# Two groups per slot for q and PV in slots 8 to 27, and the second quad's output weights prepared later

## The chip, the cores and the metric

The kernel runs on one core of a Trainium2 chip. A core has a matrix engine (PE, whose weight loads are listed apart as PEld), a vector engine (DVE), a scalar engine (ACT), a general engine (POOL), and queues that start DMA transfers (SP issues nearly all of them here). Every engine takes its instructions strictly in the order in which they were written, and waits at the head of its list until what the next instruction needs is there. The metric is the time of one execution in microseconds (us).

## The reference

One transformer block with adaptive layer norm: an attention part, a gated feed-forward part, and a modulation vector from `c`.

```python
mod = (_silu(c) @ w_mod).reshape(c.shape[0], 6, 1, -1)
h = _layernorm(x) * (1 + ca) + sa              # x: 2048 rows of 512
q = (h @ wq)                                   # 32 heads of 128
scores = q @ k.T * (128 ** -0.5)               # 8 k/v heads, the last 512 keys
o = softmax(scores) @ v
x = x + ga * (o @ wo)                          # wo: 4096 x 512
h = _layernorm(x) * (1 + cb) + sb
x = x + gb * ((_gelu(h @ w_gate) * (h @ w_up)) @ w_down)
```

All inputs are float32. The kernel computes each float32 product as three float16 matmuls: both operands are split into a high and a low half, and high·high, high·low and low·high are added up in PSUM. One such triple is called a group below.

## The kernel before

**Slots and units.** The attention part is cut into 512 slots. Slot t computes one tile of scores, 128 queries by 512 keys, for one head; four slots are a unit (one head, 512 queries), four units a set (two heads, two query blocks), and eight sets of four units make one half of the rows. The loop over t at the end of the attention part writes one slot after the other, and each slot writes to all engines.

**What a slot writes.** `scores(t)` is one group on PE into a PSUM bank `ps`; there are two such banks, so the scores of slot t need the bank that the exponentials of slot t-2 have read. `peak(t)` is the row maximum on DVE (`nm`). `expo(t)` is the exponential on ACT (`ee`), with the row sums. In odd slots ACT scales the sums of two slots (`rr`), and DVE takes their reciprocal in the slot after. `high(t-2)` on ACT writes the high half of the normalised probabilities, `low(t-3)` on DVE the low half (both called `p`), and SP then starts the DMA that transposes them into `pt`.

**What fills PE.** After the scores, a slot takes groups off a queue called `work`: q projections (`pq`, four groups for a unit), the product of probabilities and values (PV, `po`, four groups for a unit, of the unit two before), and from slot 30 on output projections (`py`). How many it takes is `EARLY[t]` for the first slots and 3 after them. In slots 8 to 27 each unit puts eight groups in the queue, so before the change its four slots take 3, 3, 2 and 0. When a `pq` or a `po` is complete, ACT writes the high half of its float16 split (`qt` or `ot`, line 747) at the start of the next slot, ahead of that slot's exponential, and DVE the low half (line 748) behind that slot's maximum. The same pair of instructions splits `w` and `k` where they are needed early.

**Banks.** Eight PSUM banks: two for `ps`, one called `qa`, and five (`acc`) that are handed round among `pq`, `po`, `py`, small sums (`pst`) and, in slots that the table `PSE` names, the exponentials `ee`; in the other slots `ee` lies in SBUF. A new tile waits for the last reader of the one that had its bank.

**Output weights.** A quad is four heads, whose rows of `wo` get one scale. `wo_items` loads each tile, lets ACT take its sum of squares (`sumsq`, line 219), lets `o_spread` turn the four sums into a scale on POOL and DVE, loads the tile again, and lets POOL multiply it and split it into halves (lines 657, 159 and 160) and SP store it. The slots are those of `WOS` (sums of squares) and `WOP` (the multiplication), counted from the quad's first set; the second quad counts from slot 32. POOL prepares the `w` tiles of each set in the same way (`set_steps`, lines 163, 159, 160 and 806).

Of the kernel before, what the change touches and what calls it, by code (L numbers as in the profile page):

```python
# [52 lines left out]
NPT = 3  # L53
NE = 6
CB = (11, 27)
PSE = dict.fromkeys((5, 7, 8, 9, 14, 18, 19, 21, 22, 23, 25, 26, 27), "acc") | dict.fromkeys((11, 15, 20, 24, 28), "qa")
EARLY = (2, 2, 0, 0, 2, 2, 0, 0)
WOS = ((6, 7, 8, 9), (-9, -8, -6, -5), (-16, -15, -14, -13))
WOP = ((17, 19, 20, 22), (10, 12, 16, 17), (-6, -4, 10, 12), (-6, -4, -3, -2))
SETPOS = (20, 14, 13, 12, 10, 8)  # L60
SETPOS2 = (18, 12, 11, 10, 9, 7)
TAIL = 12
# [3 lines left out]
def block_kernel(ctx: ExitStack, tc: tile.TileContext, x, kT, v, wq, wo, wg, wu, wd, cT, wc, wm, out):  # L66
# [8 lines left out]
    def tmp(name):  # L75
        return pool.tile([P, 512], F32, tag="e", name=name, bufs=NE)
# [7 lines left out]
    def bank(tag, name, bufs):  # L84
        return psum.tile([P, 512], F32, tag=tag, name=name, bufs=bufs)
# [7 lines left out]
    acc, moved, bg = {}, [0], []  # L93
# [61 lines left out]
    def halves(dst, src, act=False):  # L155
        if act:
            nc.scalar.activation(dst[:, 0, :], src, AF.Copy)
        else:
            nc.gpsimd.tensor_scalar(dst[:, 0, :], src, 1.0, 1.0, op0=ALU.mult, op1=ALU.mult)
        nc.gpsimd.tensor_tensor(dst[:, 1, :], src, dst[:, 0, :], op=ALU.subtract)  # L160

    def times(t, by):
        nc.gpsimd.tensor_scalar(t, t, by, 1.0, op0=ALU.mult, op1=ALU.mult)
# [15 lines left out]
    def col(name, i=0):  # L179
        return ST[name][:, i:i + 1]  # L180
# [7 lines left out]
    def little(name, n=1, bufs=4, dtype=F32):  # L188
        return small.tile([P, n], dtype, tag=name, name=name, bufs=bufs)
# [27 lines left out]
    def sumsq(out, src):  # L217
        with nc.allow_low_precision(reason="only a scale follows from it, which the margin in norm2 covers"):
            nc.scalar.activation(junk, src, AF.Square, scale=PRE, accum_out=out)
# [6 lines left out]
    def norm2(out, m, n, by, ps=None):  # L226

        ps = ps or sums(m, n)
        if n == 1:
            ts(out, ps[:, 0:1], TINY, None, ALU.max)  # L230
        elif n == 2:
            ts(out, ps[:, 0:1], TINY, ps[:, 1:2], ALU.max, ALU.add)
        else:
            nc.vector.tensor_reduce(out, ps[:, 0:n], axis=AX.X, op=ALU.add)
            pool_ts(out, out, TINY, 1.0, ALU.max)
        nc.gpsimd.tensor_tensor(out, out, half_, op=ALU.pow)  # L236
        pool_ts(out, out, by * 1.005 / PRE)

    def pool_ts(out, src, a, b=1.0, op0=ALU.mult, op1=ALU.mult):
        nc.gpsimd.tensor_scalar(out, src, a, b, op0=op0, op1=op1)  # L240

    def then(fn, d=3):

        if now[0] < 0:
            fn()
        else:
            at(("d", now[0] + d), fn)
# [29 lines left out]
    def y_scale(qd):  # L277
        pool_ts(col("ysc", qd), col("ysc", qd), col("vmax", qd), 1.0 / TOP15)

    def o_spread(qd, m, more):  # L280
        w = col("ysc", qd)
        norm2(w, m, 4, 1.0)
        pool_ts(w, w, col("gam", 0), 1.0 / TOP14)
        pool_ts(w, w, 1e-30, 1.0, ALU.max)

        def second():
            nc.vector.reciprocal(col("osc", qd), w)
            if qd == 0:
                y_scale(qd)
            more()  # L290

        then(second)
# [332 lines left out]
    def get_v():  # L625
        return pair("v16", "v16", 2)
# [7 lines left out]
    def reader(src):  # L634
        st = {}

        def load():
            st["r"] = raw("raw")
            dma(st["r"], src)

        return st, load

    def wo_items(qd, ts_, tp):
        m = {}
        for k in range(4):
            h = 4 * qd + k
            src = wo[h * P:(h + 1) * P, :]
            st, load = reader(src)
            sp, load_again = reader(src)

            def stat(st=st, k=k):
                if not m:
                    m["m"] = little("lm", 4, dtype=BF16)
                sumsq(m["m"][:, k:k + 1], st["r"])

            def parts(sp=sp, h=h):
                nc.gpsimd.tensor_tensor(sp["r"], sp["r"], m["g"], op=ALU.mult)
                WO[0, h] = get_wo()
                halves(WO[0, h], sp["r"])

            if qd == 0:
                def load_kept(st=st, sp=sp, src=src):
                    st["r"] = sp["r"] = pool.tile([P, D], F32, tag="wo", name="wor", bufs=8)
                    dma(st["r"], src)

                at(3 + k, load_kept)
                at(("w", ts_[k]), stat)
                at(("w", tp[k]), parts)
            else:
                sched(ts_[k], (load, [stat]))  # L670
                sched(tp[k], (load_again, [parts]))
            at(tp[k] + 5, lambda h=h: store(("wo", h), WO[0, h]))

        def more():
            m["g"] = pool.tile([P, D], F32, tag="gs", name="gs", bufs=1)
            pool_ts(m["g"], rows[2], col("osc", qd))

        def spread():
            o_spread(qd, m["m"], more)

        at(("w", ts_[3] + (4 if 1 < qd < 7 else 3)), spread)
# [25 lines left out]
    def v_items(g):  # L707
        st, load = reader(v[g])
        m = {}

        def stat():
            m["m"] = little("lm", 4, dtype=BF16)
            sumsq(m["m"][:, 0:1], st["r"])

        def spread():
            w = little("lw", 1, 2)
            norm2(col("vmax", g), m["m"], 1, 1.0)
            pool_ts(w, col("vmax", g), 1.0 / TOP14)
            if g:
                y_scale(g)  # L720
            then(lambda: nc.vector.reciprocal(col("vsc", g), w), 3 if g > 1 else 2)

        def parts():
            KV[0, g, 1] = get_v()
            times(st["r"], col("vsc", g))
            halves(KV[0, g, 1], st["r"])

        return load, stat, spread, parts
# [13 lines left out]
    def run(key):  # L742
        for fn in later.pop(key, []):
            fn()
# [248 lines left out]
    def expo(t):  # L993
        e = bank(PSE[t], "ee", NACC if PSE[t] == "acc" else 1) if t in PSE else tmp("ee")
        if t % 2 == 0:
            sm = small.tile([P, 2], F32, name="sm", bufs=4)
        else:
            sm = E[t - 1]["sm"]
        nc.scalar.activation(e, E[t]["ps"], AF.Exp, bias=E[t]["nm"], scale=1.0, accum_out=sm[:, t % 2:t % 2 + 1])  # L999
        E[t].update(e=e, sm=sm)  # L1000
# [217 lines left out]
    for g in range(NG):  # L1218
        half, pr = divmod(g, NPR)
        t0 = 16 * g  # L1220
        qd = pr // 2
# [21 lines left out]
        else:  # L1243
# [12 lines left out]
            if pr % 2 == 0:  # L1256
                wo_items(qd, [t0 + o + (qd == 7) for o in WOS[min(qd, 2)]], [t0 + o for o in WOP[min(qd, 2) + qd // 6]])

# [302 lines left out]
    with tc.manual_schedule():  # L1561
        begin()
        nexty, invs = [], {}
        for t in range(T + TAIL):
# [27 lines left out]
            run(("x", t))  # L1592
            for _ in range(4 if t >= T else EARLY[t] if t < len(EARLY) else 3):
                if t in (4, 5):
# [245 lines left out]
```

## Time and profile before

| | us |
|---|---|
| median of 3 runs | 1733.63 (1732.84 to 1733.82) |
| the profiled execution, and its span | 1734.19, and 1732.4 |
| PE busy in the span | 1711.2 (99%) |
| DVE, ACT, POOL busy | 1425.8 (82%), 1254.3 (72%), 1093.3 (63%) |
| scores of slot 8, of slot 28 and of slot 30 start at | 45.18, 92.28 and 98.35 |

The 1.8 us between the profiled execution and its span lie outside the recorded instructions. In a list of instructions in order of time, the first number of a row is its start from the span's start, the second its duration; a bracket at the end gives the idle time of that engine just before, and what ended it. Three matmuls of a group are listed as x3 and overlap, so that six of them, listed as 1.46 us, take 1.29 us from start to start.

### The profile page before, as it was taken

Reading aid. Unit: us, or ns where it says so; the run is one execution under the profiler, and the core shown is the slowest. Engines: PE = TensorE matmul, PEld = TensorE weight load, DVE = VectorE, ACT = ScalarE, POOL = GpSimd, SP = SyncE. Lnnn points to the kernel's source line nnn. Section 1 sums busy time; section 2 is a strip of 40 time slices with the busy share of each in tenths; the row PEclk is TensorE's granted clock in tenths of the full one; section 3 lists DMA queues with packets and bytes.
Section 4 is the critical chain, followed back from the end, with each engine's and each line's share of the span. In section 5 each row is a group of like instructions: output and inputs, shape, how many; then the busy total and the mean of one; then the engine's idle time right before and its main releaser. Section 6 shows DMA issues by size and latency. Waiting matters only on the chain.

```text
span 1732.4 us, 26343 instructions
## 1 busy us (share of the span) xinstructions
PE 1711.2 (99%) x8012; PEld 787.1 (45%) x8012; DVE 1425.8 (82%) x2476; ACT 1254.3 (72%) x2819; POOL 1093.3 (63%) x1328
## 2 busy tenths in 40 slices
PE   7999999999999999999999999999999999999998
PEld 5444444444444444444444444444444444444444
DVE  7888898988888899888888888888896788676666
ACT  6988788888888777897787777787785354455442
POOL 4879778777788884655665755747760345735424
PEclk9999999999999999999999999999999999999999
DMA  7999999999999998999999999999997556355353
GB/s 234 218 208 210 214 214 205 225 205 220 211 229 222 206 210 181 219 207 224 198 232 219 206 231 208 203 218 221 229 227 164 163 145 196 118 164 174 96 157 104
DMA packets 693454, 343.51 MB, mean 198 GB/s; under 512 B 579136, under 2 KB 602688, under 8 KB 693312
## 3 DMA queue, kind: packets, MB, share of 16 engines
q1 hardware_dynamic: 693024, 341.30, 85.4%
q8 instruction: 63, 1.03, 0.3%
q14 instruction: 79, 0.65, 0.1%
q10 hardware_dynamic: 288, 0.52, 0.1%
HBM read 137.50 MB, written 63.70 MB: 116 GB/s over the span
## 4 chain that ended last, share of the span: by engine, by line
PE 86%; DVE 5%; ACT 4%; POOL 2%; DMA 2%; issue 1%; SPq 0%; POOLq 0%; DVEq 0%; ACTq 0%
PE py L91 18%; PE po L91 17%; PE ps L91 16%; PE fa L91 8%; PE qa L91 8%; PE fc L91 4%; PE qc L91 4%; PE ya L91 3%; PE fb L91 2%; PE qb L91 2%; PE yc L91 2%; ACT ee L999 1%; DVE p L1016 1%; DVE nm L990 1%; ACT p L1011 1%
## 5 line engine op out<-in xcount | busy, mean ns | idle before, releaser
L999 ACT ACTIVATE ee<-ps,nm 128x512 f32<-128x512 f32 x512 | 349.6, 683 | 184.2 <-DVE nm L990 181.0
L1016 DVE SCALAR_TENSOR_TENSOR p<-ee,rr,p 128x512 f16<-128x512 f32 x512 | 454.1, 887 | 8.1 <-ACT p L1011 7.5
L990 DVE TENSOR_REDUCE nm<-ps 128x1 f32<-128x512 f32 x512 | 350.3, 684 | 105.7 <-PE ps L91 102.9
L91 PE MATMUL ps<-k,qt 128*128 128x512 f16 x1536 | 414.9, 379 | 3.8 <-ACT ee L999 2.5
L1011 ACT ACTIVATE p<-ee,rr 128x512 f16<-128x512 f32 x512 | 363.9, 711 | 21.9 <-DMA pt<-p 11.6
L91 PE MATMUL po<-pt,v 128*128 128x512 f16 x1536 | 372.9, 379 | 2.8 <-DVE kmax L184 1.0
L91 PE MATMUL py<-wo,ot 128*128 128x512 f16 x1536 | 371.3, 379 | 0.0
L91 PEld LDWEIGHTS <-w 128*128 128x128 f16 x2184 | 214.0, 98 | 259.7 <-issue 2.7
L91 PEld LDWEIGHTS <-v 128*128 128x128 f16 x1536 | 149.9, 98 | 185.1 <-issue 5.1
L91 PEld LDWEIGHTS <-ot 128*128 128x128 f16 x1536 | 150.3, 98 | 181.2
L91 PEld LDWEIGHTS <-qt 128*128 128x128 f16 x1536 | 145.8, 98 | 174.8 <-issue 3.3
L1320 POOL TENSOR_TENSOR fg<-fg 128x512 f32<-128x512 f32 x48 | 63.0, 1312 | 147.0 <-DVE fg L1294 144.2
L748 DVE SCALAR_TENSOR_TENSOR ot<-po,ot 128x512 f16<-128x512 f32 x128 | 87.8, 686 | 37.7 <-ACT ot L747 37.3
L1304 ACT ACTIVATE at<-fg 128x512 f16<-128x512 f32 x92 | 56.3, 626 | 80.1 <-DVE fg L1294 61.7
L999 ACT ACTIVATION_READ_ACCUMULATOR ee<-ps,nm 128x1 f32 x512 | 100.1, 195 | 0.0
L960 DVE SCALAR_TENSOR_TENSOR acc<-py,ysc,acc 128x512 f32<-128x512 f32 x128 | 94.7, 740 | 5.3 <-PE py L91 5.3
L91 PE MATMUL qa<-t,w 128*128 128x512 f16 x348 | 84.9, 379 | 0.0
L236 POOL TENSOR_TENSOR lw<-lw,half__86 128x1 f32<-128x1 f32 x39 | 25.0, 641 | 91.0 <-DVE lw L186 91.0
L91 PE MATMUL fa<-t,w 128*128 128x512 f16 x336 | 81.7, 379 | 0.1
L747 ACT ACTIVATE ot<-po 128x512 f16<-128x512 f32 x128 | 73.9, 577 | 5.0 <-PE po L91 5.0
L403 POOL TENSOR_TENSOR rs<-rs,nhalf 128x1 f32<-128x1 f32 x32 | 18.7, 586 | 92.9 <-DVE rs L397 90.0
L91 PEld LDWEIGHTS <-wo 128*128 128x128 f16 x504 | 49.3, 98 | 60.6 <-issue 1.3
(243 smaller groups left out, 2821.9 us busy)
## 6 DMA issues: line engine op xcount, KB each, us to landing
w<-kept SPq DMA_DIRECT2D x123, 256.0 KB, 3.3
wo<-kept SPq DMA_DIRECT2D x72, 256.0 KB, 3.3
kept<-stage SPq DMA_DIRECT2D x67, 256.0 KB, 3.2
raw<-in_wo SPq DMA_DIRECT2D x56, 256.0 KB, 3.2
kept<-w SPq DMA_DIRECT2D x39, 256.0 KB, 3.3
rw<-in_wq SPq DMA_DIRECT2D x38, 256.0 KB, 3.1
hs<-hf SPq DMA_DIRECT2D x32, 256.0 KB, 2.8
pt<-p SPq DMA_TRANSPOSE x512, 3.5
```

The costliest lines, as they stand in the source:

```text
L91: nc.tensor.matmul(ps, a, b, start=first and n == 0, stop=last and n == 2, skip_group_check=chain)
L236: nc.gpsimd.tensor_tensor(out, out, half_, op=ALU.pow)
L403: nc.gpsimd.tensor_tensor(st["rs"], st["rs"], nhalf, op=ALU.pow)
L747: nc.scalar.activation(t[:, 0, :], src, AF.Copy, scale=scale)
L748: return lambda: nc.vector.scalar_tensor_tensor(t[:, 1, :], src, scale, t[:, 0, :], op0=ALU.mult, op1=ALU.subtract)
L960: nc.vector.scalar_tensor_tensor(acc[ti], st["p"], by, acc[ti], op0=ALU.mult, op1=ALU.add)
L990: nc.vector.tensor_reduce(nm, E[t]["ps"], axis=AX.X, op=ALU.max, negate=True)
L999: nc.scalar.activation(e, E[t]["ps"], AF.Exp, bias=E[t]["nm"], scale=1.0, accum_out=sm[:, t % 2:t % 2 + 1])
L1011: nc.scalar.activation(p16[:, 0, :], E[t]["e"], AF.Copy, scale=E[t]["r"])
L1016: nc.vector.scalar_tensor_tensor(p16[:, 1, :], E[t]["e"], E[t]["r"], p16[:, 0, :], op0=ALU.mult, op1=ALU.subtract)
L1304: nc.scalar.activation(t[:, 0, :], g, AF.Copy)
L1320: nc.gpsimd.tensor_tensor(g[o], g[a], g[b], op=ALU.subtract)
```

## The change

`EARLY` is continued with twenty 2s: slots 8 to 27 take two groups each. `WOS` and `WOP` get other slots for the second quad: its sums of squares move from slots 23, 24, 26 and 27 to 35, 36, 38 and 39, its multiplications from 42, 44, 48 and 49 to 47, 49, 52 and 53. The second quad's `ysc` is then multiplied by `vmax` where the first's is, in `o_spread`. `PSE` names other slots; among others 6, 12, 13, 16 and 17 now have their `ee` in PSUM, and 8, 11, 14 and 15 in SBUF.

```diff
-EARLY = (2, 2, 0, 0, 2, 2, 0, 0)
+EARLY = (2, 2, 0, 0, 2, 2, 0, 0) + (2,) * 20
-PSE = dict.fromkeys((5, 7, 8, 9, 14, 18, 19, ...), "acc") | dict.fromkeys((11, 15, 20, 24, 28), "qa")
+PSE = dict.fromkeys((5, 6, 7, 9, 13, 17, 18, 19, ...), "acc") | dict.fromkeys((12, 16, 20, 24, 28), "qa")
-WOS = ((6, 7, 8, 9), (-9, -8, -6, -5), (-16, -15, -14, -13))
+WOS = ((6, 7, 8, 9), (3, 4, 6, 7), (-16, -15, -14, -13))
-WOP = ((17, 19, 20, 22), (10, 12, 16, 17), (-6, -4, 10, 12), (-6, -4, -3, -2))
+WOP = ((17, 19, 20, 22), (15, 17, 20, 21), (-6, -4, 10, 12), (-6, -4, -3, -2))
@@ o_spread, second()
             nc.vector.reciprocal(col("osc", qd), w)
-            if qd == 0:
+            if qd < 2:
                 y_scale(qd)
@@ v_items, spread()
-            if g:
+            if g > 1:
                 y_scale(g)
```

PE's order differs only up to slot 33; ACT's, DVE's, POOL's and SP's up to about slot 56. Three places show how.

ACT from the exponential of slot 22 to that of slot 25, before:

```order
L999 ACTIVATE ee,sm<-ps,nm 128x512
L1011 ACTIVATE p_1100<-ee,rr 128x512
L747 ACTIVATE ot<-po 128x512
L999 ACTIVATE ee,sm<-ps,nm 128x512
L1004 ACTIVATE rr<-sm 128x2
L1011 ACTIVATE p_1130<-ee,rr 128x512
L219 ACTIVATE junk,lm<-raw 128x512
L999 ACTIVATE ee,sm<-ps,nm 128x512
L1011 ACTIVATE p_1149<-ee,rr 128x512
L747 ACTIVATE k<-raw,ksc 128x512
L219 ACTIVATE junk,lm<-raw 128x512
L999 ACTIVATE ee,sm<-ps,nm 128x512
```

and the same stretch now:

```order
L999 ACTIVATE ee,sm<-ps,nm 128x512
L1011 ACTIVATE p_1089<-ee,rr 128x512
L999 ACTIVATE ee,sm<-ps,nm 128x512
L1004 ACTIVATE rr<-sm 128x2
L1011 ACTIVATE p_1117<-ee,rr 128x512
L747 ACTIVATE ot<-po 128x512
L999 ACTIVATE ee,sm<-ps,nm 128x512
L1011 ACTIVATE p_1143<-ee,rr 128x512
L747 ACTIVATE k<-raw,ksc 128x512
L999 ACTIVATE ee,sm<-ps,nm 128x512
```

The two sums of squares are gone, and the `ot` split stands ahead of the exponential of slot 24, no longer of slot 23.

DVE from the maximum of slot 23 to the `k` split of slot 25, before (`p_1149` is the low half of slot 22):

```order
L990 TENSOR_REDUCE nm<-ps 128x1
L748 SCALAR_TENSOR_TENSOR ot<-po,ot 128x512
L1016 SCALAR_TENSOR_TENSOR p_1100<-ee,rr,p_1100 128x512
L990 TENSOR_REDUCE nm<-ps 128x1
L1007 RECIPROCAL rr<-rr 128x2
L1016 SCALAR_TENSOR_TENSOR p_1130<-ee,rr,p_1130 128x512
L990 TENSOR_REDUCE nm<-ps 128x1
L1016 SCALAR_TENSOR_TENSOR p_1149<-ee,rr,p_1149 128x512
L748 SCALAR_TENSOR_TENSOR k<-raw,ksc,k 128x512
```

and now (`p_1143` is the low half of slot 22):

```order
L990 TENSOR_REDUCE nm<-ps 128x1
L1016 SCALAR_TENSOR_TENSOR p_1089<-ee,rr,p_1089 128x512
L990 TENSOR_REDUCE nm<-ps 128x1
L748 SCALAR_TENSOR_TENSOR ot<-po,ot 128x512
L1007 RECIPROCAL rr<-rr 128x2
L1016 SCALAR_TENSOR_TENSOR p_1117<-ee,rr,p_1117 128x512
L990 TENSOR_REDUCE nm<-ps 128x1
L1016 SCALAR_TENSOR_TENSOR p_1143<-ee,rr,p_1143 128x512
L748 SCALAR_TENSOR_TENSOR k<-raw,ksc,k 128x512
```

The `ot` split moved from an odd slot to an even one, where the reciprocal and a low half stand behind it. Slots 12, 16 and 20 show the same.

POOL around slots 48 to 54, where it makes the `w` tiles of the fifth set (`w_2145` before, `w_2143` now), before:

```order
L657 TENSOR_TENSOR raw<-raw,gs 128x512
L159 TENSOR_SCALAR wo<-raw 128x512
L160 TENSOR_TENSOR wo<-raw,wo 128x512
L240 TENSOR_SCALAR qsc<-lt 128x1
...
L806 TENSOR_TENSOR rw<-rw 128x256 x4
L159 TENSOR_SCALAR w_2145<-rw 128x512
L160 TENSOR_TENSOR w_2145<-rw,w_2145 128x512
```

and now:

```order
L806 TENSOR_TENSOR rw<-rw 128x256 x4
L657 TENSOR_TENSOR raw<-raw,gs 128x512
L159 TENSOR_SCALAR wo<-raw 128x512
L160 TENSOR_TENSOR wo<-raw,wo 128x512
L657 TENSOR_TENSOR raw<-raw,gs 128x512
L159 TENSOR_SCALAR wo<-raw 128x512
L160 TENSOR_TENSOR wo<-raw,wo 128x512
L159 TENSOR_SCALAR w_2143<-rw 128x512
L160 TENSOR_TENSOR w_2143<-rw,w_2143 128x512
```

Two of the second quad's four tiles, which stood ahead of all of that set's steps, now stand between them, ahead of its second `w` tile.

More of the change, by code (lines that the diff above doesn't have):

```diff
@@ L55 @@
 CB = (11, 27)
-PSE = dict.fromkeys((5, 7, 8, 9, 14, 18, 19, 21, 22, 23, 25, 26, 27), "acc") | dict.fromkeys((11, 15, 20, 24, 28), "qa")
-EARLY = (2, 2, 0, 0, 2, 2, 0, 0)
-WOS = ((6, 7, 8, 9), (-9, -8, -6, -5), (-16, -15, -14, -13))
-WOP = ((17, 19, 20, 22), (10, 12, 16, 17), (-6, -4, 10, 12), (-6, -4, -3, -2))
+PSE = dict.fromkeys((5, 6, 7, 9, 13, 17, 18, 19, 21, 22, 23, 25, 26, 27), "acc") | dict.fromkeys((12, 16, 20, 24, 28), "qa")
+EARLY = (2, 2, 0, 0, 2, 2, 0, 0) + (2,) * 20
+WOS = ((6, 7, 8, 9), (3, 4, 6, 7), (-16, -15, -14, -13))
+WOP = ((17, 19, 20, 22), (15, 17, 20, 21), (-6, -4, 10, 12), (-6, -4, -3, -2))
 SETPOS = (20, 14, 13, 12, 10, 8)
```

## The prediction

> **What bounds the kernel now.** I read the page's engine table first, then stretches of the span side by side, to find where PE is not full.
>
> ```profile
> PE 1711.2 (99%) x8012; PEld 787.1 (45%) x8012; DVE 1425.8 (82%) x2476; ACT 1254.3 (72%) x2819; POOL 1093.3 (63%) x1328
> ...
> 45.18:92.28 47.10, 43.67 (x206) 20.16 (x206) 39.35 (x75) 42.87 (x105) 38.97 (x54) 0.96 1.07 220
> 83.57:87.00 3.43, 3.43 (x10) 1.31 (x9) 3.43 (x7) 2.47 (x8) 3.25 (x4) 0.53 1.18 306
> 92.28:98.35 6.07, 5.46 (x25) 2.27 (x24) 5.43 (x10) 5.90 (x17) 1.65 (x2) 1.00 0.86 189
> 100.00:120.00 20.00, 20.00 (x97) 9.08 (x95) 17.89 (x37) 17.21 (x42) 14.33 (x25) 1.00 1.00 217
> ```
>
> The stretches give length, then the busy time of PE, PEld, DVE, ACT and POOL, then the clock granted to PE. PE is the bound from slot 30 on. The changed slots 8 to 27 are the first long row: there PE is idle 47.10 - 43.67 = 3.43 us, and for 3.43 us more it runs at 0.53 of its clock, which costs 3.43 x 0.47 = 1.6 us. Slots 28 and 29 hold another 6.07 - 5.46 = 0.61. The change removes no matmul, so the most that it can win is 3.43 + 1.6 + 0.61 = 5.6 us, 0.32%. The waits of PE and the chain of waits, both cut to this part, say who holds it up:
>
> ```profile
> PE ps L91 <- ACT ee L999: 2.4, 3, 1.9
> ...
> by line: ACT ee L999 16.3%; issue 15.3%; ACT p L1011 14.0%; DVE nm L990 11.4%; DVE p L1016 8.1%; ACT junk L219 5.5%; ACT qt L747 5.0%; DVE w L748 3.6%; ACT ot L747 3.5%; DVE qt L748 3.1%; ACT rr L1004 2.7%; PE po L91 2.2%; DVE gam L192 1.5%
> ...
> 82.82 0.95 PE L91 MATMUL ps<-k,qt 128*128 128x512 f16 x3 [1.86 <-ACT ee L999]
> 97.06 1.46 PE L91 MATMUL po<-pt,v 128*128 128x512 f16 x6 [0.61 <-DVE nm L990]
> ```
>
> PE itself has 2.2% of that chain. ACT and DVE alternate: maximum, exponential, halves, and PE waits for a score bank. The number to forecast is therefore when the last late step comes, the PV group at 97.06 in slot 29, since PE is full behind it. The named releaser `nm` was long done there; the step is the transposed `p` of slot 23, whose low half is the last of its inputs:
>
> ```profile
> 92.27 0.73 DVE L1016 SCALAR_TENSOR_TENSOR p<-ee,rr,p 128x512 f16<-128x512 f32 x1
> ...
> 93.06 1.23 SPq L1020 DMA_TRANSPOSE pt<-p  x1
> ```
>
> From the start of that low half to the PV group it is 97.06 - 92.27 = 4.79 us, which the change leaves as it is.
>
> **The pacing and the `ot` split, slots 8 to 20.** The same groups run in other slots; at 0.65 us a group (half of the 1.29 of six matmuls) PE loses and gains nothing. What moves is `ot`. On ACT it now delays an even exponential, and on DVE it stands ahead of the reciprocal and a low half. Prices, from start to start:
>
> ```profile
> 92.97 0.59 ACT L747 ACTIVATE ot<-po 128x512 f16<-128x512 f32 x1
> 93.45 0.63 ACT L219 ACTIVATE junk<-raw 128x512 f16<-128x512 f32 x1
> ...
> 84.06 0.68 DVE L990 TENSOR_REDUCE nm<-ps 128x1 f32<-128x512 f32 x1
> 84.66 0.67 DVE L748 SCALAR_TENSOR_TENSOR ot<-po,ot 128x512 f16<-128x512 f32 x1
> 85.26 0.73 DVE L1016 SCALAR_TENSOR_TENSOR p<-ee,rr,p 128x512 f16<-128x512 f32 x1
> ...
> 74.33 1.42 DVE L1016 SCALAR_TENSOR_TENSOR p<-ee,rr,p 128x512 f16<-128x512 f32 x1
> 76.47 1.55 DVE L1016 SCALAR_TENSOR_TENSOR p<-ee,rr,p 128x512 f16<-128x512 f32 x1
> 79.21 0.74 DVE L1016 SCALAR_TENSOR_TENSOR p<-ee,rr,p 128x512 f16<-128x512 f32 x1
> ```
>
> ACT's half takes 93.45 - 92.97 = 0.48, DVE's 85.26 - 84.66 = 0.60. Walked in the way that slots 22 to 29 are below, the slots up to the exponential of slot 16 take both in. In slot 17 DVE's `ot`, a wait for ACT's half ahead of it included, makes the maximum late by about 0.55 (bounds: 0, if the slack holds, and 0.60); in slot 20 ACT's half puts the exponential 0.48 back (0 to 0.48). `PSE` gives back more: the low halves of slots 16 and 17 read `ee` from SBUF and took 1.42 and 1.55, now they read PSUM and should take 0.74 like the next one: 1.42 + 1.55 - 2 x 0.74 = 1.49 (0 to 1.49; I take all, both stand on the chain). Slots 14 and 15, 8 and 11 go the other way and get longer low halves, ahead of slot 16, where the walk finds room for them (0 to 0.8 each; I take 0). So the exponential of slot 22 starts 0.55 + 0.48 - 1.49 = -0.46, some 0.4 us, earlier than before.
>
> **Slots 22 to 29.** Here the chain can be walked instruction by instruction, with the orders shown above.
>
> ```profile
> 84.77 0.66 ACT L999 ACTIVATE ee<-ps,nm 128x512 f32<-128x512 f32 x1 [0.93 <-DVE nm L990]
> ...
> 88.72 0.63 ACT L219 ACTIVATE junk<-raw 128x512 f16<-128x512 f32 x1
> 89.33 0.66 ACT L999 ACTIVATE ee<-ps,nm 128x512 f32<-128x512 f32 x1
> 90.14 0.20 ACT L1004 ACTIVATE rr<-sm 128x2 f32<-128x2 f32 x1
> 90.25 0.67 ACT L1011 ACTIVATE p<-ee,rr 128x512 f16<-128x512 f32 x1
> 90.82 0.68 ACT L747 ACTIVATE qt<-pq,qsc 128x512 f16<-128x512 f32 x1
> ...
> 81.53 0.75 DVE L748 SCALAR_TENSOR_TENSOR qt<-pq,qsc,qt 128x512 f16<-128x512 f32 x1 [0.98 <-ACT qt L747]
> 82.19 0.15 DVE L1007 RECIPROCAL rr<-rr 128x2 f32<-128x2 f32 x1
> 82.27 0.73 DVE L1016 SCALAR_TENSOR_TENSOR p<-ee,rr,p 128x512 f16<-128x512 f32 x1
> 82.92 1.22 DVE L748 SCALAR_TENSOR_TENSOR w<-rw,wsc,w 128x512 f16<-128x512 f32 x1
> 89.21 1.47 DVE L748 SCALAR_TENSOR_TENSOR k<-raw,ksc,k 128x512 f16<-128x512 f32 x1
> 90.61 0.68 DVE L990 TENSOR_REDUCE nm<-ps 128x1 f32<-128x512 f32 x1
> ```
>
> DVE's `qt` starts at 81.1 instead of 81.53, and the reciprocal, the low half, `w` and the maximum of slot 23 follow as before (84.06 - 81.53 = 2.53), so the maximum starts near 83.65 and the exponential 84.77 - 84.06 = 0.71 behind it, 84.35. ACT then takes 0.81 to `rr` (89.33 to 90.14), 0.11 to the high half, 0.57 to `ot` (90.25 to 90.82) and 0.48 for it: `ot` starts at 85.84, the exponential of slot 24 at 86.3. Its place ahead of that exponential was a sum of squares'. DVE's `ot` can't start before ACT's ends, 85.84 + 0.59 = 86.4; behind it, 0.60, stand the reciprocal (0.08), the low half (0.65) and the maximum of slot 25, at 87.75. Here is the new wait: 0.7 us of what the removed sums of squares free on ACT is lost behind `ot`. The exponential of slot 25 comes at 88.45, 0.9 earlier than 89.33. The low half of slot 22 follows at 88.35 and `k` at 89.0; `k` takes 90.61 - 89.21 = 1.40, so the maximum of slot 26 comes at 90.4, only 0.2 earlier. Then 0.60 for it, 0.66 for `qt`, 0.08: the low half of slot 23 starts at 91.75, and with 4.79 the PV group starts at 96.55, against 97.06: **0.5 us earlier**. PE's own work would let it start at 96.15 (score 28 at 92.25, below, and six groups), so this step still ends last. Its bounds: 96.15 (0.9 earlier), and 0.5 later if the 1.49 of `PSE` are halved and both `ot` prices stay.
>
> PE waits meanwhile twice for a bank whose last reader is a low half, in slots 22 and 26; the second begins near 87.7 (the exponential of slot 24 ends at 86.3 + 0.66, and score 26 takes 0.65 behind it) and ends with the low half of slot 22, 88.35 + 0.73 = 89.1, so about 1.35 us. Idle time and half clock together come out as before by score 28 (92.25 against 92.28).
>
> **The sums of squares in slots 35 to 39 and the multiplications.** Four at 0.61 (88.72 to 89.33) on ACT.
>
> ```profile
> 118.30 0.69 ACT L999 ACTIVATE ee<-ps,nm 128x512 f32<-128x512 f32 x1 [1.32 <-DVE nm L990]
> ...
> 121.74 0.81 PE L91 MATMUL ps<-k,qt 128*128 128x512 f16 x3
> ...
> 148.79 1.27 POOL L657 TENSOR_TENSOR raw<-raw,gs 128x512 f32<-128x512 f32 x1
> 152.29 1.27 POOL L657 TENSOR_TENSOR raw<-raw,gs 128x512 f32<-128x512 f32 x1
> 167.12 1.16 POOL L160 TENSOR_TENSOR w<-rw,w 128x512 f16<-128x512 f32 x1
> ...
> 176.85 1.46 PE L91 MATMUL qa<-t,w 128*128 128x512 f16 x6
> ```
>
> ACT is busy 17.21 of 20 there and takes three of the four in that stretch, 1.8: full but for 1 us. The exponential at 118.30 had waited 1.32 and ends at 119.0; the score that needs its bank starts at 121.74, so 2.7 us cover a delay of 0.61 a slot. Without that cover it would cost up to 4 x 0.61 = 2.4; I take 0. Their loads and stores move along on SP, one with each tile, and I take 0 for them; if a load is late, POOL is, which the next lines bound.
>
> POOL is tighter. A tile's multiplication and split take 152.29 - 148.79 = 3.5 us. Two tiles now stand ahead of the `w` tile that was done at 167.12 + 1.16 = 168.28 and that PE first reads at 176.85: 8.6 us, less 2 x 3.5 = 7.0, leaves 1.6. I take 0 (bounds: 0, and a wait of up to some 3 us if POOL runs as much later than that).
>
> **Sum.** -0.5. The profiled execution, 1734.19, is 0.56 above the median; -0.5 makes it 1733.7, and the median **1733.1**.
>
> **A rule to weigh.** After the idle 1.86 us of slot 24 the clock was halved:
>
> ```profile
> 80.16:83.57 3.41, 1.55 (x7) 0.57 (x7) 2.43 (x5) 3.41 (x8) 3.23 (x4) 0.97 1.07 121
> ```
>
> PE was busy 1.55 of 3.41 us ahead of the 3.43 at 0.53. The bank wait of slot 26, 1.35 us, is near that. The Trainium skill, "TensorE: Matmul & The Clock Gate", section "Why this matters for your kernels", asks for no idle gap above about 3 us. By it no wait of this size could halve the clock, and the sum stays -0.5; by this trace, where 1.86 us did, a second dip costs 1.6 and the sum is +1.1. The measurement decides, so the dip stays a case.
>
> **The rivals.**
>
> A second dip: the wait in slot 26 halves the clock in slots 26 to 29, where PE has no slack to speak of: -0.5 + 1.6 = +1.1, 1734.7. For it the row above, against it that 1.35 is under 1.86. It stays within what counts as no change.
>
> Faster: the waits and the dip go away, because two groups a slot keep PE busy while ACT and DVE catch up. Of the removed work the chain holds three sums of squares; the rows of the first and the last are
>
> ```profile
> 86.36 0.29 ACT junk L219
> ...
> 93.56 0.61 ACT junk L219 x2
> ```
>
> With the second, as long as the last, 0.29 + 0.61 + 0.61 = 1.5, and the low halves' 1.49: 3.0; with all idle time gone 5.6. So 1728.0 to 1730.6, 1729.3 in the middle. It decides if `ot` finds DVE free, so that maxima follow their scores at once. Against it: DVE is busy 39.35 of the 47.10 us, and `ot` now leads the reciprocal.
>
> Slower: POOL's two tiles. If POOL comes to that `w` tile more than 1.6 us later than worked out, PE, which has no other cover there, waits one for one; from 1.86 us of idle on the half clock adds 1.6. At 4 us later: 2.4 + 1.6 - 0.5 = +3.5, 1737.1. For it: the 3.5 us come from one pair of rows, and each tile waits for its load. Against it: POOL is busy 14.33 of 20 us in the stretch from 100 to 120, so it can make up a lag. It decides from a lag of about 4.
>
> **How the numbers follow.** A change of 0.2%, 3.5 us, is about what a measurement of this kernel can tell from none. Forecast, 0.42: 1732.7 to 1734.1. Second dip, 0.16: up to 1734.7 or a little above. Faster, 0.22: 1728.0 to 1730.6, nearly all of it (0.20) beyond 0.2%, since without `ot`'s price the dip should go too. Slower, 0.20: 1737.1 on, taken as beyond. So faster 0.20, same 0.60, slower 0.20. The range 1729.0 to 1738.0 leaves out the best end of the faster case and the worst of POOL's, about 2 in 10. The forecast's own range with the dip is 1732.7 to 1735.
>
> **What would show it.** Right: the exponential of slot 25 near 88.5, `k` behind it, the low half of slot 23 near 91.8, PV in slot 29 near 96.6, slots 30 on at 2.59 us each; low halves of slots 16 and 17 at 0.74; PE full from 100 to 200. Wrong: score 28 far from 92.3, a granted clock of 0.5 after slot 26, PE waiting on `w` near 177 to 180, or exponentials of slots 36 to 40 that hold a score bank.

## The result

The changed kernel takes **1736.55 us** (median of 20 runs) against 1732.66 us for the kernel before (20 runs): ratio **1.0021, interval 1.0014 to 1.0027**, some 3.6 us slower by the ratio. One of its 20 runs took 1994.1 us at a granted clock of 0.85 and is not in the ratio. The prediction was 0.5 us faster (1733.1, from the 1733.63 known then); the time lies inside its range and on the wrong side.

The profiled execution took 1736.56 us, with a span of 1734.8. Its table of engines shows no engine with more work:

```profile
PE 1710.0 (99%) x8010; PEld 786.4 (45%) x8012; DVE 1421.2 (82%) x2476; ACT 1254.3 (72%) x2819; POOL 1093.0 (63%) x1328
```

So time was lost in waits. Stretches of the span (length, busy time of PE, PEld, DVE, ACT and POOL, granted clock, DMA share, GB/s) show two places. Before:

```profile
45.00:100.00 55.00, 50.95 (x238) 23.39 (x239) 45.76 (x86) 50.16 (x124) 41.25 (x56) 0.97 1.05 218
160.00:180.00 20.00, 20.00 (x95) 9.13 (x94) 17.66 (x32) 15.16 (x35) 18.32 (x24) 1.00 1.00 203
180.00:200.00 20.00, 20.00 (x97) 9.04 (x95) 16.64 (x32) 16.65 (x43) 12.67 (x19) 1.00 1.03 227
```

After:

```profile
45.00:100.00 55.00, 48.51 (x231) 22.34 (x230) 44.68 (x84) 47.07 (x115) 41.11 (x55) 1.00 0.96 204
160.00:180.00 20.00, 19.45 (x92) 8.61 (x89) 14.45 (x25) 12.32 (x28) 18.49 (x23) 1.00 0.99 208
180.00:200.00 20.00, 18.91 (x88) 8.43 (x89) 18.24 (x33) 16.56 (x42) 15.84 (x21) 1.00 0.85 191
```

In the first stretch PE is idle 6.5 us instead of 4.1, although the half clock is gone. The second place is new: between 160 and 200 PE was always full, and now loses 1.6 us; DVE and ACT each lose about 3 us between 160 and 180. Here is what stood in the way, on DVE and ACT around slots 58 and 59:

```profile
174.73 0.74 DVE L1016 SCALAR_TENSOR_TENSOR p<-ee,rr,p 128x512 f16<-128x512 f32 x1
178.44 0.17 DVE L287 RECIPROCAL osc<-ysc 128x1 f32<-128x1 f32 x1 [2.97 <-POOL ysc L240]
178.52 0.68 DVE L771 TENSOR_TENSOR qb<-s,qb 128x512 f32<-128x512 f32 x1
179.10 0.68 DVE L990 TENSOR_REDUCE nm<-ps 128x1 f32<-128x512 f32 x1
...
179.29 0.69 ACT L747 ACTIVATE qt<-qb,qsc 128x512 f16<-128x512 f32 x1 [3.72 <-DVE qb L771]
179.87 0.68 ACT L999 ACTIVATE ee<-ps,nm 128x512 f32<-128x512 f32 x1
```

DVE stands 2.97 us at a reciprocal of one column, `osc` of the *third* quad (line 287, in `o_spread`), because POOL has not made the `ysc` it reads. Behind it in DVE's list wait the sum `qb` and the maximum of the next slot, behind them ACT's `qt` and the exponential. Before, that reciprocal came with no idle time ahead of it, and the exponential of slot 59 at 175.59:

```profile
174.16 0.15 DVE L287 RECIPROCAL osc<-ysc 128x1 f32<-128x1 f32 x1
...
175.59 0.68 ACT L999 ACTIVATE ee<-ps,nm 128x512 f32<-128x512 f32 x1
```

POOL's list says why. Before, the `ysc` steps of the third quad ran from 168.37 to 171.1:

```profile
168.37 0.55 POOL L240 TENSOR_SCALAR ysc<-ysc 128x1 f32<-128x1 f32 x1
...
170.85 0.23 POOL L240 TENSOR_SCALAR ysc<-ysc 128x1 f32<-128x1 f32 x1
```

After, they follow the two `wo` tiles and the `w` tile, and end at 178.4:

```profile
173.19 1.16 POOL L160 TENSOR_TENSOR wo<-raw,wo 128x512 f16<-128x512 f32 x1
...
175.01 1.47 POOL L160 TENSOR_TENSOR w<-rw,w 128x512 f16<-128x512 f32 x1
176.56 0.23 POOL L240 TENSOR_SCALAR ysc<-ysc 128x1 f32<-128x1 f32 x1
...
178.17 0.23 POOL L240 TENSOR_SCALAR ysc<-ysc 128x1 f32<-128x1 f32 x1
```

### The profile page after: what moved, and what is told of

Read it like the earlier page. It is cut to its first block, busy times and chain, and to the rows that moved or that the text cites. A ratio compares the mean times of both kernels' runs of the same rounds, so it can differ in the third digit from the quotient of the medians.

```text
span 1734.8 us, 26329 instructions
## 1 busy us (share of the span) xinstructions
PE 1710.0 (99%) x8010; PEld 786.4 (45%) x8012; DVE 1421.2 (82%) x2476; ACT 1254.3 (72%) x2819; POOL 1093.0 (63%) x1328
## 4 chain that ended last, share of the span: by engine, by line
PE 83%; DVE 5%; ACT 4%; POOL 4%; issue 2%; DMA 1%; POOLq 0%; DVEq 0%; ACTq 0%
PE py L91 18%; PE po L91 16%; PE ps L91 15%; PE fa L91 8%; PE qa L91 7%; PE fc L91 4%; PE qc L91 4%; PE ya L91 3%; PE fb L91 2%; PE qb L91 2%; PE yc L91 2%; ACT ee L999 1%; DVE p L1016 1%; ACT p L1011 1%; DVE nm L990 1%
## 5 line engine op out<-in xcount | busy, mean ns | idle before, releaser
L1016 DVE SCALAR_TENSOR_TENSOR p<-ee,rr,p 128x512 f16<-128x512 f32 x512 | 449.5, 878 | 7.0 <-ACT p L1011 6.7
L1687 DVE SCALAR_TENSOR_TENSOR yt<-ya,dyc,yt 128x512 f32<-128x512 f32 x82 | 60.3, 745 | 19.5 <-PE ya L91 19.4
```

Of the source, the lines that this page charges most:

```text
L1016: nc.vector.scalar_tensor_tensor(p16[:, 1, :], E[t]["e"], E[t]["r"], p16[:, 0, :], op0=ALU.mult, op1=ALU.subtract)
L1687: nc.vector.scalar_tensor_tensor(YT[key], ps, by, YT[key], op0=ALU.mult, op1=ALU.add)
```

## The experiments

Each kernel was timed beside the kernel before. The traces can be compared more finely than the times: the table gives the start of an exponential less its start before, in us, counted from slot 8 (ahead of it the executions differ by -0.8 to +1.0 us, which is left out). Kernels with the same order up to slot 45, such as "output weights" and "weights, `osc` late", differ by up to 0.5 us there, so one trace does not tell less than that from chance.

| kernel | ratio (interval) | slot 22 | 30 | 45 | 58 | 64 | 128 |
|---|---|---|---|---|---|---|---|
| changed | 1.0021 (1.0014 to 1.0027) | +1.2 | +1.4 | +1.4 | +1.9 | +5.4 | +4.1 |
| pacing and PSE | 1.0010 (1.0001 to 1.0018) | +1.2 | +1.6 | +1.1 | +1.1 | +1.1 | +1.1 |
| output weights | 1.0015 (1.0006 to 1.0024) | 0.0 | -0.1 | -0.1 | +0.5 | +4.0 | +2.6 |
| `osc` late | 1.0012 (1.0004 to 1.0021) | +1.2 | +1.2 | +1.2 | +1.8 | +3.3 | +2.8 |
| tiles early | 1.0035 (1.0021 to 1.0049) | +1.2 | +1.2 | +1.0 | +5.7 | +6.4 | +5.7 |
| pacing, `ot` behind | 0.9991 (0.9982 to 1.0000) | -0.3 | -0.4 | -0.7 | -0.7 | -0.7 | -0.7 |
| the same again | 0.9995 (0.9986 to 1.0004) | -0.3 | -0.4 | -0.7 | -0.7 | -0.8 | -0.8 |
| pacing, PSE of before | 1.0008 (0.9999 to 1.0016) | +1.0 | +1.9 | +1.4 | +1.4 | +1.4 | +1.4 |
| weights, `osc` late | 0.9999 (0.9990 to 1.0008) | 0.0 | -0.5 | -0.5 | -0.4 | +1.0 | +0.5 |
| both repairs | 0.9994 (0.9985 to 1.0003) | -0.3 | -1.4 | -1.4 | -1.3 | +0.2 | -0.3 |
| before, `ot` behind | 0.9992 (0.9983 to 1.0000) | -0.6 | -1.5 | -1.6 | -1.6 | -1.6 | -1.6 |
| repairs, tiles late | 0.9988 (0.9979 to 0.9997) | -0.3 | -1.3 | -1.3 | -1.3 | -0.6 | -1.1 |

**The two halves of the change.** First the pacing with its `PSE`, then the output weights, each alone in the kernel before:

```diff
-EARLY = (2, 2, 0, 0, 2, 2, 0, 0)
+EARLY = (2, 2, 0, 0, 2, 2, 0, 0) + (2,) * 20
-PSE = dict.fromkeys((5, 7, 8, 9, 14, 18, 19, ...), "acc") | dict.fromkeys((11, 15, 20, 24, 28), "qa")
+PSE = dict.fromkeys((5, 6, 7, 9, 13, 17, 18, 19, ...), "acc") | dict.fromkeys((12, 16, 20, 24, 28), "qa")
```

> The kernel before with the new pacing and the new PSE alone. Theory A (the third quad's scale: POOL comes to its steps late, and DVE's reciprocal `osc` stands 2.97 us at the head of DVE's list in slot 58): only the part of slots 8 to 30 is left, about +1.35 us between score 8 and score 30, ratio 1.0003 to 1.0010. Theory C (the pacing carries nearly all): +3 us or more, ratio 1.0015 or more.

```diff
-WOS = ((6, 7, 8, 9), (-9, -8, -6, -5), (-16, -15, -14, -13))
+WOS = ((6, 7, 8, 9), (3, 4, 6, 7), (-16, -15, -14, -13))
-WOP = ((17, 19, 20, 22), (10, 12, 16, 17), (-6, -4, 10, 12), (-6, -4, -3, -2))
+WOP = ((17, 19, 20, 22), (15, 17, 20, 21), (-6, -4, 10, 12), (-6, -4, -3, -2))
...
-            if qd == 0:
+            if qd < 2:
                 y_scale(qd)
...
-            if g:
+            if g > 1:
                 y_scale(g)
```

> The kernel before with the second quad's output weights moved, and nothing else. Theory A: DVE waits some 3 us for POOL ahead of `osc` in slot 58, the exponentials behind it come about 3 us late and win 1 to 1.5 us back up to slot 96: ratio 1.0010 to 1.0017. Theory C: no more than +0.5 us, ratio under 1.0004, perhaps below 1 since four sums of squares leave slots 23 to 27.

1734.49 and 1735.13 us, against 1732.65: each half costs on its own, and the two add up to about the whole (+1.0 and +1.5 of +2.1 thousandths). The second has the same wait, to the hundredth:

```profile
177.47 0.16 DVE L287 RECIPROCAL osc<-ysc 128x1 f32<-128x1 f32 x1 [2.97 <-POOL ysc L240]
```

DVE also waits for the second quad's own `osc`, in slot 46; the changed kernel has the same wait:

```profile
140.90 0.17 DVE L287 RECIPROCAL osc<-ysc 128x1 f32<-128x1 f32 x1 [0.76 <-POOL ysc L240]
```

Theory C falls; theory A's numbers hold for both.

**Is it the reciprocal, or POOL's lateness?** In the changed kernel the third quad's `osc` comes two slots later on DVE, with its first two tiles two slots and one slot later; POOL stays as late:

```diff
-        then(second)
+        then(second, 5 if qd == 2 else 3)
-WOP = (..., (-6, -4, 10, 12), ...)
+WOP = (..., (-4, -3, 10, 12), ...)
```

> The changed kernel with the third quad's `osc` two slots later on DVE (slot 60; its first two tiles two slots and one slot later). POOL is as late as in the changed kernel. Theory A: DVE's wait of 2.97 us shrinks to under 0.3, and the ratio falls to that of the pacing alone, 1.0003 to 1.0010. Theory B (what hurts is POOL's lateness itself, through the `w` tile that PE reads and through the loads of `rw` that stand on SP ahead of transposes): the ratio stays at 1.0015 or above, with PE waits in slots 58 to 62.

```profile
181.50 0.15 DVE L287 RECIPROCAL osc<-ysc 128x1 f32<-128x1 f32 x1
```

No idle time is left ahead of it, and the exponential of slot 64 comes 2.1 us earlier than in the changed kernel (+3.3 for +5.4). 1734.97 us, ratio 1.0012, between the two forecasts: 1.6 us won, less than the 2.97 that DVE stood. Between slots 58 and 64 another 1.5 us are lost. So theory A holds for the larger part up to slot 64, and for less than half up to slot 128 (the loss between slots 45 and 128 falls from 2.7 to 1.6 us); theory B holds for a rest. The rest can be followed in the trace. SP's two loads of `rw` wait for the buffers that POOL's late `w` tiles read, 2.5 us each, and go out some 5 us later than before (172.16 and 175.63 there). Behind the first stands a transpose: its low half was complete at 175.82, it starts at 177.30, and PE waits for the `pt`:

```profile
SPq L97 <- POOL w L160: 2.5, 1, 2.5
...
176.86 0.33 SPq L97 DMA_DIRECT2D rw<-in_wq  x1
177.30 1.23 SPq L1020 DMA_TRANSPOSE pt<-p  x1
181.06 0.33 SPq L97 DMA_DIRECT2D rw<-in_wq  x1
...
180.67 0.82 PE L91 MATMUL po<-pt,v 128*128 128x512 f16 x3 [0.87 <-DMA pt<-p]
```

The changed kernel has this wait too (0.86 at 180.32), more than half of the 1.6 us that PE loses there; before the change PE has none between 160 and 200.

**Tiles ahead of the set's steps again.**

```diff
-WOP = (..., (15, 17, 20, 21), ...)
+WOP = (..., (14, 15, 16, 17), ...)
```

> The changed kernel with the second quad's multiplications in slots 46 to 49 instead of 47, 49, 52 and 53, so ahead of the fifth set's steps again. Theory A: POOL is at the third quad's scale about as early as before the change, no wait ahead of `osc`, ratio 1.0003 to 1.0010. If the four tiles now make the set's own scale late instead, a wait of DVE or POOL at the `lr` and `qsc` steps shows near 150 us and the ratio stays above 1.0010.

A miss by far: 1739.82 us. The third quad's scale is early again, but four tiles in a row make the fifth set's first `w` tile late, and PE has to wait for it, with half the clock behind the wait (six matmuls in 2.46 us):

```profile
165.72 2.46 PE L91 MATMUL qa<-b,w 128*128 128x512 f16 x6 [2.39 <-POOL w L160]
```

This is what the prediction's slower rival described, at the set's first `w` tile; in the changed kernel itself it does not occur.

**The pacing: where `ot` stands on DVE.** In the changed kernel DVE waits for ACT's half of `ot` in slots 16, 20, 24 and 28 (0.89 in the last, too):

```profile
67.51 0.69 DVE L748 SCALAR_TENSOR_TENSOR ot<-po,ot 128x512 f16<-128x512 f32 x1 [0.76 <-ACT ot L747]
76.16 0.69 DVE L748 SCALAR_TENSOR_TENSOR ot<-po,ot 128x512 f16<-128x512 f32 x1 [0.80 <-ACT ot L747]
87.38 0.69 DVE L748 SCALAR_TENSOR_TENSOR ot<-po,ot 128x512 f16<-128x512 f32 x1 [0.89 <-ACT ot L747]
```

So, on top of the pacing and `PSE` alone:

```diff
-        first(split_post(oT[u], ps, ACC))
+        (soon if now[0] < 28 else first)(split_post(oT[u], ps, ACC))
```

> The pacing and PSE alone, with DVE's half of `ot` in slots 12, 16, 20, 24 and 28 behind the reciprocal and the low half instead of ahead of them; ACT's order is the same. Theory P1 (in the even slots DVE stands waiting for ACT's `ot`, 0.76 to 0.89 us each, with the reciprocal and a low half queued behind): the waits shrink to under 0.2, score 30 comes 0.8 to 1.5 us earlier than with the pacing alone, ratio 0.9998 to 1.0005. Theory P2 (the time goes into low halves and splits that POOL stretches, 1.49 to 1.71 us): no more than 0.3 us gained, ratio near 1.0010.

1731.68 us, and 1732.37 when it was run again:

> The pacing and PSE with `ot` behind the low half once more, on this chip beside the two others: ratio 0.9985 to 0.9997 again, below 1.0 with its interval, if it beats both kernels.

The two traces agree to 0.1 us in the table up to slot 128: 1.8 us earlier than the pacing alone at slot 45, more than either theory gave. The waits at `ot` are gone. The second interval takes in 1.0, so that it beats the kernel before is likely, not shown. The control is the same line in the kernel before:

> The kernel before, its pacing and PSE untouched, with DVE's half of `ot` behind the low half up to slot 28. There `ot` falls into odd slots, which have no reciprocal, and DVE waits only 0.2 to 0.3 us for it. Theory P1 (the even slots make the wait dear): no more than 0.5 us gained, ratio 0.9997 to 1.0002. If the order of these two is worth the same at any pacing: ratio about 0.9985 to 0.9990.

1731.51 us, ratio 0.9992: **a miss** for theory P1. The order of `ot` and the low half is worth nearly as much in the old pacing (1.6 us at slot 45, against 1.8), where DVE waited for `ot` only 0.2 to 0.3 us. So the dear even slots (theory P1) are not what makes the pacing slow; with the order repaired in both, the pacing still costs 0.9 us at slot 45 (-0.7 against -1.6). Which of its moves does, these runs don't split. What the order does can be read in DVE's groups by shape, from 45 to 98 us. Before:

```profile
L748 DVE SCALAR_TENSOR_TENSOR w<-rw,wsc,w 128x512 f16<-128x512 f32 x2 | 2.0, 980 | 0.0
L748 DVE SCALAR_TENSOR_TENSOR k<-raw,ksc,k 128x512 f16<-128x512 f32 x1 | 1.5, 1472 | 0.0
```

Before, with `ot` behind the low half:

```profile
L748 DVE SCALAR_TENSOR_TENSOR w<-rw,wsc,w 128x512 f16<-128x512 f32 x2 | 1.5, 748 | 0.1
L748 DVE SCALAR_TENSOR_TENSOR k<-raw,ksc,k 128x512 f16<-128x512 f32 x1 | 0.7, 746 | 0.0
```

`k` and one of the two `w` splits take 0.75 instead of 1.47 and 1.22; the low halves of slots 16 and 17 take 1.10 and 0.96 instead of 1.42 and 1.55. The last section shows how that hangs on POOL.

**The PSE table.** The pacing with the `PSE` of before:

> The pacing alone with the PSE of before, so the exponentials of slots 16 and 17 lie in SBUF again, those of 14 and 15 in PSUM. If the PSE table is worth what the prediction gave it (1.49 us), this is 1 to 1.5 us slower than pacing and PSE together: ratio about 1.0018. If the long low halves only move with it (theory P2: POOL's tensor-tensor instructions stretch whatever DVE reads from SBUF beside them), within 0.4 us of it: ratio about 1.0010.

1734.61 us, ratio 1.0008; the pacing with its own `PSE` had 1.0010. The table is worth 0.2 to 0.3 us at slots 30 to 128, hardly more than chance, not 1.49. It does what it says (the low half of slot 17 takes 1.66 here), but other passes become long: in the changed kernel the low halves of slots 11 and 14, whose `ee` the table put into SBUF, and the `w` split behind slot 17's.

```profile
76.74 1.66 DVE L1016 SCALAR_TENSOR_TENSOR p<-ee,rr,p 128x512 f16<-128x512 f32 x1
```

```profile
63.21 1.56 DVE L1016 SCALAR_TENSOR_TENSOR p<-ee,rr,p 128x512 f16<-128x512 f32 x1
69.57 1.49 DVE L1016 SCALAR_TENSOR_TENSOR p<-ee,rr,p 128x512 f16<-128x512 f32 x1
...
77.49 1.71 DVE L748 SCALAR_TENSOR_TENSOR w<-rw,wsc,w 128x512 f16<-128x512 f32 x1
```

The first fence is the pacing with the old table, the second the changed kernel. Before the change those two low halves took 0.73 each, and the `w` split

```profile
77.95 0.74 DVE L748 SCALAR_TENSOR_TENSOR w<-rw,wsc,w 128x512 f16<-128x512 f32 x1
```

**Repairs.** The output weights alone, with both `osc` later, then the whole change with that and with `ot` behind, then that with the second quad's tiles at (15, 17, 24, 25), the last two in slots 56 and 57:

```diff
-        then(second)
+        then(second, {1: 4, 2: 6}.get(qd, 3))
-WOP = (..., (15, 17, 20, 21), (-6, -4, 10, 12), ...)
+WOP = (..., (15, 17, 20, 21), (-3, -2, 10, 12), ...)
```

> The moved output weights without the pacing, with the second quad's `osc` one slot later and the third quad's three slots later on DVE (slots 46 and 61; the third quad's first tiles in 61 and 62). Theory A: both waits for POOL at `osc` are gone, and what is left is the effect of four sums of squares less in slots 23 to 27: 0 to -0.5 us, ratio 0.9995 to 1.0003. Theory B (POOL's lateness itself, or the transposes behind late loads on SP): ratio 1.0008 or more.

> The changed kernel with both repairs, `ot` behind the low half in the even slots up to 28 and both `osc` later. By theories A and P1 the +3.6 us go: ratio 0.9995 to 1.0005. By P2 with A, 1.0008 to 1.0012 is left.

> Both repairs, and the second quad's last two multiplications in slots 56 and 57 instead of 52 and 53, so behind the fifth set's `w` tiles and the third quad's scale on POOL. Theory B for what is left of the moved weights (POOL's late `w` tiles hold up the two `rw` loads on SP, with transposes behind them; 1.5 us lost in slots 60 to 64): the loads go out at their old time, the exponential of slot 64 keeps the 2 us won by slot 58, ratio 0.9985 to 0.9992. Otherwise as with both repairs, 0.9994.

1733.08, 1732.37 and **1731.35** us; the last, 0.9988 (0.9979 to 0.9997), is the one version whose interval lies wholly below both kernels, 5.2 us under the change as it was made. It is not shown to beat the kernel before with `ot` behind (0.9992, intervals overlap), which needs one changed line. By ratio theory A's forecast came in the first, the second lies just under its range, and theory B's in the third. In the first two the exponentials still lose 1.4 and 1.5 us between slots 58 and 64, and PE waits 0.9 for `pt`. With the tiles behind the `w` tiles that loss is 0.7, the two loads go out early, and PE is all but full again:

```profile
170.47 0.53 SPq L97 DMA_DIRECT2D rw<-in_wq  x1
174.25 0.53 SPq L97 DMA_DIRECT2D rw<-in_wq  x1
...
160.00:180.00 20.00, 20.00 (x95) 9.07 (x94) 17.53 (x30) 14.29 (x33) 18.40 (x23) 1.00 0.92 194
180.00:200.00 20.00, 19.93 (x95) 9.07 (x94) 17.42 (x32) 16.02 (x42) 18.43 (x23) 1.00 0.95 226
```

That fits theory B for the rest, though the move brings the `w` tiles and the scale on POOL's list forward together, so the loads are not shown to be its only way; and its forecast, that nothing would be lost by slot 64, did not come in full.

## Why the prediction was wrong

**The multiplications: the step that failed.** The prediction took 0 for POOL, because the `w` tile kept 1.6 us of slack. That held, in part by luck: the tile was done at 175.01 + 1.47 = 176.5, some 8.2 us later than before and not 7.0, but PE came 1.1 later too, and its first product with the tile started at 177.99 without a wait. But the list of those who wait for POOL was cut off there. The third quad's `ysc` steps stand behind the same tiles, and DVE waits for them at the head of its list; SP's loads of `rw` wait for the `w` tiles, with transposes behind them. Measured: 2.97 us of DVE, +3.5 us of exponentials between slots 58 and 64 (1.9 to 5.4), some 1.3 of it won back by slot 128. `osc` moved two slots takes back 2.1 of the 3.5, and 1.3 at slot 128 (4.1 to 2.8). The second quad's own `osc` cost another 0.6 at slot 46; with `osc` later that is gone. The tiles moved behind the `w` tiles take back 0.8 more at slot 128 (-1.1 against -0.3). The slower rival had the right place and nearly the right time, 1737.1, but the wrong victim, and so too small a chance (0.20). That its time came near is luck: neither PE's wait at `w` nor the half clock, which made it up, occurred.

**The pacing, the second step that failed.** Forecast: the exponential of slot 22 0.4 us earlier; measured, counted from slot 8, 1.2 later.
- `ot` ahead of the reciprocal: the waits were foreseen and came, at the forecast size. The exponential of slot 17 is 1.1 us late with `ot` ahead and 0.6 with `ot` behind, so its price is the 0.55 of the forecast; in slot 20 it was 0.4 (0.48).
- `PSE`, -1.49: mis-sized. The table gave 0.2 to 0.3 us. The two low halves did fall to 0.74. But the prediction took 0 for slots 11 and 14, which go the other way: their low halves rose from 0.73 to 1.56 and 1.49, and the first makes slot 17 late by another 0.6 (1.1 with the new table, 0.5 with that of before). A `w` split rose from 0.74 to 1.71.
- The sums of squares: removing them won 0.4 us at slot 25, then `k` (1.63) took it back, much as walked. In the kernel with the weights alone the exponential of slot 28 was 1 us earlier, and 0.1 at slot 30: PE's half clock and the PV group of slot 29 stood behind it. So what they free is worth little there, as forecast. With `ot` behind, it is worth 0.6 to 0.7 at slot 45 (-0.7 in two traces without their move, -1.4 and -1.3 in two with it).
- PV in slot 29 started at 97.72 (98.4 if the 0.7 us ahead of slot 8 are left out), not 96.55.

**What was right.** The sums of squares in slots 35 to 39 cost nothing (+1.4 at slot 30 and at slot 45), nor did the `w` tile. There was no second dip of the clock, and the faster case did not come. The reason given against it, `ot` ahead of the reciprocal, is part of it: with `ot` behind, 1.8 us came back, short of the 3.0 to 5.6 of that case. The first dip went away, and no time was won by it: ACT and DVE set the pace there, and PE idled 2.4 us more.

## What to carry to other kernels

When an instruction is moved on an in-order engine, list everything behind it on that engine, down to the one-column steps, and for each the engine that waits for it and what stands behind that wait; the slack is that of the first to be late, and it was not the tile. A saving read off long instructions is a saving only if their cause goes; where they are long because of another engine's work beside them, the length can move to another instruction. The order of two instructions on a busy engine was worth 1.6 to 1.8 us here, more than the 0.5 forecast for the change, so it pays to try it in both kernels.

## What the runs showed of the hardware

Between 45 and 98 us DVE's splits and low halves of 512 columns take 0.67 to 0.75 us or up to 1.73, and which of the `k` and `w` splits are long follows where they start beside POOL's two-input instructions (TENSOR_TENSOR). In the 13 traces, 26 of the 27 long ones, 0.88 us or more, started while such an instruction had 0.3 us or more to go; for the 12 short ones it was at most 0.12. Before, `k` started 0.23 us behind one of them and took 1.47, until 0.54 us after that one's end. With `ot` behind the low half it started 0.08 ahead, took 0.75, and POOL's took 1.69 instead of 1.16:

```profile
88.98 1.16 POOL L384 TENSOR_TENSOR t<-s,t 128x512 f16<-128x512 f32 x1
89.21 1.47 DVE L748 SCALAR_TENSOR_TENSOR k<-raw,ksc,k 128x512 f16<-128x512 f32 x1
...
87.51 0.75 DVE L748 SCALAR_TENSOR_TENSOR k<-raw,ksc,k 128x512 f16<-128x512 f32 x1
87.59 1.69 POOL L384 TENSOR_TENSOR t<-s,t 128x512 f16<-128x512 f32 x1
```

The long `w` split of the changed kernel, 1.71, started 0.11 us behind POOL's and ended 0.55 us after it. So a shift of a tenth of a microsecond can decide which of the two is long. The Trainium skill, "SBUF — State Buffer", section "Who interferes with whom", says that a DVE instruction with two SBUF inputs contends with a GpSimd (POOL) instruction that reads SBUF. The rows agree: the long ones read both inputs from SBUF, and the `qt` split, which reads one from PSUM, takes 0.75 in every kernel here.

Idle time of much the same length halved the clock in one kernel and not in another. With the pacing alone, PE waited 1.71 us ahead of this row, and ran the six matmuls in 2.72 us; the granted clock from 80 to 84 us was 0.59:

```profile
80.91 2.72 PE L91 MATMUL po<-pt,v 128*128 128x512 f16 x6 [1.71 <-DVE p L1016]
...
80.00:84.00 4.00, 3.09 (x8) 1.13 (x8) 3.02 (x7) 3.73 (x9) 3.74 (x5) 0.59 1.07 182
```

In the changed kernel the same wait was 1.73 us, and the clock stayed full:

```profile
80.51 1.46 PE L91 MATMUL po<-pt,v 128*128 128x512 f16 x6 [1.73 <-DVE p L1016]
...
80.00:84.00 4.00, 3.49 (x17) 1.60 (x17) 3.02 (x6) 3.83 (x9) 3.82 (x4) 1.00 0.96 110
```

So a wait of this size has no fixed price. The Trainium skill, "TensorE: Matmul & The Clock Gate", section "What's actually happening", says that the window in which activity is judged runs freely and does not start with the kernel. These two rows fit that, though no run here shows it to be the reason; they do not fit the limit of about 3 us that the prediction weighed.
